# Projections from 128-row slices of x, transposed one piece at a time, and the leading maxima moved into the loop

## The chip, the core and the metric

The kernel runs on one core of a Trainium2 chip. Its engines each work through a queue of their own in order: TensorE (PE, with its weight loads shown as PEld), VectorE (DVE), ScalarE (ACT), GpSimd (POOL) and SyncE (SP), which here only issues transfers. The metric is the device time of one execution in microseconds; lower is better.

## The reference

Two independent halves, laid side by side in the output. The first is a state-space convolution: a long filter `K` is built from complex powers, and the input `u` is convolved with it by an FFT. The second is multi-head attention with 16 heads of 28 over 2048 positions.

```python
P = exp((A * dt[:, None])[:, :, None] * arange(2048))      # 448 x 256 x 2048, complex
K = 2 * einsum("dn,dnl->dl", C, P).real
a = irfft(rfft(u.T, 4096) * rfft(K, 4096))[:, :2048].T + u * D_skip

q, k, v = split_heads(x @ wqkv)       # x is 2048 x 448, wqkv is 448 x 1344
p = softmax(q @ k.T * 28 ** -0.5)
b = merge_heads(p @ v) @ wo
return concatenate([a, b], -1)
```

All numbers are float32.

## The kernel before

The kernel has a preamble and a loop.

The preamble makes q, k and v from x, and at the same time the seeds of the convolution's filter. x is cut in four quarters of 512 rows (`CQ`). For each quarter, `load_x` fetches two tiles `xn` (of three in all), `transposes` turns them on PE, and 12 jobs follow: eight `qk_proj` (four groups of heads, k and q each) and four `v_proj`. The width 448 is summed in four pieces of `CK` = 112 rows. PE multiplies in a fast float32 form, so each operand is split in a high and a low part. ACT copies the transposed piece from the PSUM tile `pt` (two buffers) into `xh`, rounded; DVE subtracts that from `pt` and writes the rest to `xl`. The weights are split in the same way (`w_g`, which lies in the memory that `khat` takes later, and `vh`, `vl`). A job adds up high times high, low weight times high x, and high weight times low x, for four pieces: twelve products into one PSUM bank `pm` (three banks in turn). After it ACT and DVE evacuate the bank into `hl` (or `vst`, or, for the last quarter's q, into the memory of `xn`), and SP stores it to DRAM. For k of the first two quarters there is a difference more, `kb` and `dhl`.

`seeds` makes the filter's seeds in eight rounds on ACT, DVE and POOL, with a few transposes (`pn`) on PE. The list `slots` sets how jobs and seed stages alternate as they are written down, 48 jobs in 37 slots (`PW`). In the preamble a planner then sets the order on each queue by its own costs (`KEPT["p"]` is empty); from the loop on every queue keeps the order as written (`KEPT["a"]`).

At the preamble's end, group 0's keys are loaded back as `khat` (and differences of keys as `kdif`), unit 0's queries as `qhat`, and the row maxima of unit 0 are taken. A unit is one group of four heads and one quarter of the queries; there are 16, and 16 steps of 128 keys each, so 256 steps. `max_put` sends the negated maxima `mh` into spare rows of `qhat`, so that the score products subtract them; ACT issues that transfer for unit 0.

Each step of the loop does, in the order of `ORDER`, four score products `pss` with their exponentials `p` on ACT, four products for the maxima of the next unit (`m0` to `m3`, `max_mm`), the product of p and v of the step before (`po`), and pieces of the convolution's work. A maximum's four products end in a ReLU `rl` on ACT for the first and a reduction on DVE for each of the other three. The loop runs `LEAD` = 3 steps ahead with its maxima; those three steps' twelve products stand between unit 0's maxima and the first step:

```python
for i in range(LEAD):
    for kc in range(4):
        max_mm(1, i, kc)
```

All instructions are recorded through one helper, so the profile puts them all on line 75; its rows are told apart by the tiles' names.

Of the kernel before, what the change touches and what calls it, by code (L numbers as in the profile page):

```python
# [18 lines left out]
D = 448  # L19

H = 16
DH = 28
# [2 lines left out]
CQ = 512  # L25
NQ = L // CQ
NK = L // 128
CK = 112
NCK = D // CK
SCALE = DH ** -0.5  # L30
NU = G * NQ
NS = NU * NK
# [6 lines left out]
SP, SH, PW, E3 = 4, 3, 37, 8  # L39
UG = (2, 2, 4)  # L40
PS = 1
SGB, XB, XL = 2, 5, 4
K0, KP, KD, UP = 0, 3.5, 4, 3
A0, A1 = 26, 31

# [45 lines left out]
def body(ctx, tc, a, out):  # L91
# [134 lines left out]
    with ExitStack() as st:  # L226
# [12 lines left out]
        def load_x(c):  # L239
            xs = x[c * CQ:(c + 1) * CQ, :].rearrange("(t p) d -> p t d", p=128)  # L240
            for h in range(2):
                xns[c, h] = y_p.tile([128, 2, CQ], F32, name="xn", bufs=3)[:, :, :D]
                nc.sync.dma_start(xns[c, h], xs[:, 2 * h:2 * h + 2, :])

        first = lambda o: (o // 4) * DF + (o % 4) * (JF // 4)
        nats = {}
# [47 lines left out]
                nc.vector.tensor_scalar(dt_all[:, i, :], dt_ps, f, None, op0=ALU.mult)  # L294

        load_x(0)
        w_g = k0_t[:CK].rearrange("p g (i s k h e) -> p i s k g h e", i=2, s=2, k=NCK, h=HG)
        vh = y_p.tile([CK, NCK, D], F32R, name="vh")
        vl = y_p.tile([CK, NCK, D], F32R, name="vl")
        nc.gpsimd.memset(k0_t[:CK].rearrange("p g (n e) -> p (g n) e", e=32)[:, :, DH:].bitcast(F32), 0.0)  # L300
# [4 lines left out]
        wns = []  # L305
        for i in range(2):
            wn = t_p.tile([128, 3, LV, BO * 16], F32, name="tri", bufs=2).rearrange("p t k h -> p (t k h)")
            wn = wn[:CK, :2 * 3 * D].rearrange("p (k s d) -> p k s d", k=2, s=3)
# [164 lines left out]

        def qk_proj(c, s, g):
            pp = w_tile()
            n = 0
            for k in range(NCK):
                for i, x_ in ((0, xh), (1, xh), (0, xl)):
                    nc.tensor.matmul(pp, w_g[:, i, s, k, g].rearrange("p h e -> p (h e)"), x_[k],
                                     start=n == 0, stop=n == 3 * NCK - 1)  # L480
                    n += 1

            def evac():
                if c == NQ - 1 and s == 0:
                    hl = y_p.tile([128, 2, CQ], F32, name="xn", bufs=3).bitcast(F32R)
                else:
                    hl = x_p.tile([128, 2, CQ], F32R, name="hl", bufs=3)
                th, tl = hl[:, 0], hl[:, 1]
                if s == 1:
                    nc.scalar.activation(th, pp, AF.Identity, bias=kones)  # L490
                    nc.vector.scalar_tensor_tensor(tl, pp, kones, th.bitcast(F32), op0=ALU.add, op1=ALU.subtract)
                else:
# [12 lines left out]
                nc.sync.dma_start((k_d[g][:, :, c * CQ:(c + 1) * CQ] if s == 1 else q_d[g][c]).rearrange("i p l -> p i l"),  # L505
                                  hl.bitcast(F32))
            return evac

        def v_proj(c, t):
            pp = w_tile()  # L510
            n = 0
            ts = slice(t * 128, (t + 1) * 128)
            for k in range(NCK):
                for w_, x_ in ((vh, xh), (vl, xh), (vh, xl)):
                    nc.tensor.matmul(pp[:, :D], x_[k][:, ts], w_[:, k, :], start=n == 0, stop=n == 3 * NCK - 1)
                    n += 1

            def evac():
                vs = vst[t % 2]
                nc.scalar.activation(vs[:, :, :DH], pp[:, :D].rearrange("p (h e) -> p h e", e=DH), AF.Copy)  # L520
                nc.sync.dma_start(v_d[c][:, :, t], vs.rearrange("p (g h) e -> p g (h e)", g=G))
            return evac

        work = []
        for c in range(NQ):
            jobs = [lambda c=c, s=s, g=g: qk_proj(c, s, g) for g in range(G) for s in (1, 0)]
            v_jobs = [lambda c=c, t=t: v_proj(c, t) for t in range(4)]
# [512 lines left out]
    def vec():  # L1040
        if powers["g"]:
            powers["g"].popleft()()

    prev = None
    for s in range(NS):
        u, kt = divmod(s, NK)
        sm = s + NK + LEAD
        if s == 12 * NK:
            k0_st.close()
            f_p["s", 0] = f_p["s", 1] = pool(f0_st, "f0_p", side="right")  # L1050
            f_ready["s", 0], f_ready["s", 1] = s, NS
# [20 lines left out]
        for op in ORDER:  # L1072
# [96 lines left out]
```

## Time and profile before

| | us |
|---|---|
| median of 3 runs (lowest to highest) | 1278.88 (1276.07 to 1279.31) |
| the profiled execution | 1278.37 |
| its span, first to last instruction | 1276.6 |
| PE busy in the span | 1223.9 (96%) |
| ACT, DVE, POOL busy | 967.5, 923.0, 846.2 |

Busy time counts an instruction from its start to its end. PE's products overlap one another, so a busy PE can still take more; how often products start tells more than how long one is. In the rows of the profile, `out<-in` are tiles, `[2.65 <-DVE xl L75]` means that the engine had stood idle for 2.65 us and what released it, and x4 means four instructions in a row. In the rows of waits stand the total in us, how often, and the longest.

### The profile page before, as it was taken

To read this page: it belongs to the slowest core of one execution; us is meant where nothing else is said; L and a number is where in the kernel's file an instruction comes from. 1 tells how busy PE (TensorE), PEld (TensorE's weight loads), DVE (VectorE), ACT (ScalarE), POOL (GpSimd) and SP (SyncE) were. 2 spreads that over 40 slices of the span, in tenths; PEclk is the share of its full clock that TensorE was granted. 3 is DMA by queue.
4 is the path that set the end of the run, shared out by engine and by line. 5 is a ranking of instruction groups with operands and counts; after the bars stand their busy time and mean duration, and the time that the engine had idled before them with its cause. 6 is when DMAs were issued, how large, how long until landed. Compare 5 with 4: busy or idle time off the path is not lost.

```text
span 1276.6 us, 33328 instructions
## 1 busy us (share of the span) xinstructions
PE 1223.9 (96%) x12641; PEld 699.3 (55%) x12641; DVE 923.0 (72%) x2106; ACT 967.5 (76%) x2162; POOL 846.2 (66%) x728
## 2 busy tenths in 40 slices
PE   7789887999999999999999999999999999999997
PEld 5667664555555555555555555555555545544433
DVE  6788866877777877877788888888897645645111
ACT  6878765788888888888878888888887666656452
POOL 2666750897788888878599999989995222324321
PEclk9889999899999999999999999999999999999999
DMA  7768699446564645375633133422324533657666
GB/s 216 244 223 288 233 304 346 113 93 186 160 149 113 168 119 168 113 235 167 176 94 104 49 88 97 154 81 71 88 54 156 179 131 135 204 170 228 198 170 167
DMA packets 200089, 205.36 MB, mean 161 GB/s; under 512 B 95992, under 2 KB 158520, under 8 KB 197880
## 3 DMA queue, kind: packets, MB, share of 16 engines
q1 hardware_dynamic: 199400, 202.63, 52.6%
q8 instruction: 100, 1.64, 0.5%
q10 hardware_dynamic: 528, 0.59, 0.2%
q14 instruction: 61, 0.50, 0.1%
HBM read 120.73 MB, written 82.18 MB: 159 GB/s over the span
## 4 chain that ended last, share of the span: by engine, by line
PE 75%; DVE 8%; POOL 6%; ACT 4%; issue 3%; DMA 3%; SPq 0%; ACTq 0%; POOLq 0%; DVEq 0%
PE pm L75 43%; PE pss L75 16%; PE po L75 16%; POOL e L75 2%; DVE tri L75 1%; ACT rl L75 1%; POOL qhat L75 1%; DVE mx L75 1%; DVE sg L75 1%; POOL eu L75 1%; ACT tri L75 1%; DVE px L75 1%; DVE qhat L75 1%; DVE hl L75 1%; DMA sd<-qhat 1%
## 5 line engine op out<-in xcount | busy, mean ns | idle before, releaser
L75 ACT ACTIVATE p<-pss 128x512 f32<-128x512 f32 x1024 | 561.0, 610 | 112.5 <-PE pss L75 107.2
L75 PE MATMUL pss<-qhat,khat 128*128 128x512 f32 x1024 | 403.2, 400 | 1.5 <-ACT p L75 1.4
L75 DVE TENSOR_REDUCE mx<-pm 128x1 f32<-128x512 f32 x480 | 308.6, 684 | 109.1 <-PE pm L75 107.2
L75 PE MATMUL pm<-khat,qhat 128*128 128x512 f32 x749 | 325.9, 438 | 6.4 <-ACT rl L75 4.2
L75 POOL TENSOR_TENSOR e<-e,sdb 128x256 f32<-128x256 f32 x168 | 201.8, 1201 | 110.6 <-ACT e L75 101.2
L75 PE MATMUL po<-p,v 128*32 128x512 f32 x2048 | 269.1, 594 | 0.0
L75 POOL TENSOR_TENSOR e<-e,eu 128x256 f32<-128x256 f32 x168 | 248.2, 1477 | 13.2
L75 PEld LDWEIGHTS pm<-khat,qhat 128*128 128x128 f32 x749 | 141.0, 189 | 201.9 <-ACT p L75 47.8
L75 DVE CUSTOM_DVE_ANT_0 rl<-pm,rl 128x512 f32<-128x512 f32 x259 | 178.3, 689 | 72.1 <-ACT rl L75 69.1
L75 PEld LDWEIGHTS pss<-qhat,khat 128*128 128x128 f32 x1024 | 190.6, 189 | 46.7 <-issue 10.8
L75 POOL TENSOR_TENSOR eu<-e,sdb 128x256 f32<-128x256 f32 x168 | 201.9, 1202 | 0.0
L75 POOL TENSOR_TENSOR p<-pr,pr 64x448 f32<-64x448 f32 x64 | 73.2, 1144 | 158.2 <-PE pm L75 132.8
L75 ACT ACTIVATE rl<-pm 128x512 f32<-128x512 f32 x259 | 156.6, 606 | 14.0 <-PE pm L75 8.4
L75 DVE TENSOR_TENSOR g<-g,zg 128x128 f32<-128x128 f32 x392 | 162.2, 414 | 3.4
L75 PE MATMUL pm<-kdif,qhat 128*128 128x512 f32 x249 | 100.5, 403 | 4.3 <-DVE xn L75 2.4
L75 PE MATMUL pm<-xh,khat 112*128 112x512 f32 x256 | 87.3, 425 | 4.9 <-DVE hl L75 1.8
L75 DVE TENSOR_TENSOR zg<-g,zg 128x128 f32<-128x128 f32 x224 | 88.0, 393 | 5.1
L75 PEld LDWEIGHTS pm<-e,g 128*32 128x32 f32 x3584 | 57.2, 109 | 43.4 <-issue 17.1
L75 DVE TENSOR_TENSOR pr<-pm,ub 128x448 f32<-128x448 f32 x64 | 37.0, 620 | 56.4 <-PE pm L75 42.0
L75 PE MATMUL pm<-e,g 128*32 128x64 f32 x3584 | 73.0, 222 | 1.8 <-POOL e L75 1.8
L75 ACT ACTIVATE y<-pm 128x448 f32<-128x448 f32 x48 | 26.5, 553 | 58.2 <-PE pm L75 36.2
L75 ACT ACTIVATE ub<-pm 128x224 f32<-128x224 f32 (+1 forms) x96 | 38.8, 449 | 39.7 <-PE pm L75 37.3
(134 smaller groups left out, 1461.8 us busy)
## 6 DMA issues: line engine op xcount, KB each, us to landing
sdb<-sd SPq DMA_DIRECT2D x55, 336.0 KB
qhat<-q SPq DMA_DIRECT2D x64, 256.0 KB
khat<-k SPq DMA_DIRECT2D x64, 256.0 KB
sd<-sg SPq DMA_DIRECT2D x8, 1456.0 KB
k<-hl SPq DMA_DIRECT2D x16, 512.0 KB
mw<-in_mw SPq DMA_DIRECT2D x16, 512.0 KB
sd<-qhat SPq DMA_DIRECT2D x8, 896.0 KB
yu_d<-ub SPq DMA_DIRECT2D x64, 112.0 KB
```

The costliest lines, as they stand in the source:

```text
L75: i = f(*args, **kw)
```

## The change

Three things are changed.

The width of 448 is now cut in three pieces of 128 rows and a rest of 64 (`TL`). The rest stands twice in a fourth piece of 128 rows: `load_x` fetches the last 64 columns of x a second time, behind the others, and the weights' last 64 rows are loaded twice. In the transposed fourth piece the lower half keeps the high part and the upper half is overwritten with the low part, so that one product with the high weights does high and low x together. A job then has 3 + 3 + 3 + 2 = 11 products.

The transposes of quarter c + 1 are written down piece by piece with jobs 7 to 10 of quarter c (`TJ`), not all ahead of the quarter's first job; only quarter 0 keeps them there. So x of two quarters is held at once: seven tiles a quarter, of which even quarters take five from the buffers of `v` (which the loop fills later), and the others come from `xt` (nine buffers, as many as `xh` and `xl` had together).

The leading maxima are no longer made ahead of the loop. `next_max` counts products, and a fifth one is made at the end of each step until the lead is reached, after step 11.

```diff
-CK = 112
-NCK = D // CK
+CK = 128
+NCK = 4
+TL = D - 3 * CK
-SGB, XB, XL = 2, 5, 4
+SGB, XT = 2, 9
+TJ = 7
...
             for h in range(2):
-                xns[c, h] = y_p.tile([128, 2, CQ], F32, name="xn", bufs=3)[:, :, :D]
-                nc.sync.dma_start(xns[c, h], xs[:, 2 * h:2 * h + 2, :])
+                xns[c, h] = y_p.tile([128, 2, CQ], F32, name="xn", bufs=3)
+                for d, n, at in ((0, D, 0), (D - TL, TL, D)):
+                    nc.sync.dma_start(xns[c, h][:, :, at:at + n], xs[:, 2 * h:2 * h + 2, d:d + n])
...
         for k in range(NCK):
-            nc.sync.dma_start(wns[k], wqkv[k * CK:(k + 1) * CK, :].rearrange("p (s d) -> p s d", s=3))
+            for p in range(1 if k < NCK - 1 else 2):
+                n = CK if k < NCK - 1 else TL
+                nc.sync.dma_start(wns[k][p * TL:p * TL + n], wqkv[k * CK:k * CK + n, :].rearrange("p (s d) -> p s d", s=3))
...
-        def transposes(c):
-            for k in range(NCK):
-                pt = ps_t.tile([128, CQ], F32, name="pt")[:CK]
+        def x_tile(c):
+            if c % 2:
+                return x_p.tile([128, CQ], F32R, name="xt", bufs=XT)
+            if n_x[0] < 5:
+                n_x[0] += 1
+                return v_p.tile([128, NK // NQ, HG, 32], F32, name="v", bufs=5).rearrange("p t h e -> p (t h e)").bitcast(F32R)
+            n_x[0] = (n_x[0] + 1) % 7
+            return x_p.tile([128, CQ], F32R, name="xt", bufs=XT)
+
+        def transposes(c, ks):
+            for k in ks:
+                pt = ps_t.tile([128, CQ], F32, name="pt")
                 for t in range(4):
                     nc.tensor.transpose(pt[:, t * 128:(t + 1) * 128], xns[c, t // 2][:, t % 2, k * CK:(k + 1) * CK], ident)
-                xh[k] = x_p.tile([CK, CQ], F32R, name="xh", bufs=XB)
-                xl[k] = x_p.tile([CK, CQ], F32R, name="xl", bufs=XL)
-                nc.scalar.activation(xh[k], pt, AF.Copy)
-                nc.vector.tensor_tensor(xl[k], pt, xh[k].bitcast(F32), ALU.subtract)
+                xh[c, k] = x_tile(c)
+                nc.scalar.activation(xh[c, k], pt, AF.Copy)
+                if k < NCK - 1:
+                    xl[c, k] = x_tile(c)
+                    nc.vector.tensor_tensor(xl[c, k], pt, xh[c, k].bitcast(F32), ALU.subtract)
+                else:
+                    nc.vector.tensor_tensor(xh[c, k][TL:], pt[TL:], xh[c, k][TL:].bitcast(F32), ALU.subtract)
...
-                for i, x_ in ((0, xh), (1, xh), (0, xl)):
-                    nc.tensor.matmul(pp, w_g[:, i, s, k, g].rearrange("p h e -> p (h e)"), x_[k],
+                for i, x_ in ((0, xh), (1, xh), (0, xl))[:3 if k < NCK - 1 else 2]:
+                    nc.tensor.matmul(pp, w_g[:, i, s, k, g].rearrange("p h e -> p (h e)"), x_[c, k],
...
-            jobs[0] = (lambda c, f: lambda: (transposes(c), f())[1])(c, jobs[0])
+            if c == 0:
+                jobs[0] = (lambda f: lambda: (transposes(0, range(NCK)), f())[1])(jobs[0])
             if c + 1 < NQ:
                 jobs[1] = (lambda c, f: lambda: (load_x(c + 1), f())[1])(c, jobs[1])
+                for k in range(NCK):
+                    jobs[TJ + k] = (lambda c, k, f: lambda: (transposes(c + 1, [k]), f())[1])(c, k, jobs[TJ + k])
...
-    for i in range(LEAD):
-        for kc in range(4):
-            max_mm(1, i, kc)
...
+    n_max = [4 * NK]
+
+    def next_max(end=None):
+        n = n_max[0]
+        if n < 4 * NS and (end is None or n < end):
+            n_max[0] += 1
+            max_mm(*divmod(n // 4, NK), n % 4)
...
+        lead = 4 * sm + 4 if s >= 4 * LEAD else 4 * (s + NK + 1) + s + 1
...
-            elif sm < NS:
-                max_mm(sm // NK, sm % NK, int(op[1]))
+            else:
+                next_max()
+        next_max(lead)
```

More of the change, by code (lines that the diff above doesn't have):

```diff
@@ L296, in body @@
         load_x(0)
-        w_g = k0_t[:CK].rearrange("p g (i s k h e) -> p i s k g h e", i=2, s=2, k=NCK, h=HG)
+        w_g = k0_t.rearrange("p g (i s k h e) -> p i s k g h e", i=2, s=2, k=NCK, h=HG)
         vh = y_p.tile([CK, NCK, D], F32R, name="vh")
         vl = y_p.tile([CK, NCK, D], F32R, name="vl")
-        nc.gpsimd.memset(k0_t[:CK].rearrange("p g (n e) -> p (g n) e", e=32)[:, :, DH:].bitcast(F32), 0.0)
+        nc.gpsimd.memset(k0_t.rearrange("p g (n e) -> p (g n) e", e=32)[:, :, DH:].bitcast(F32), 0.0)
         vst = [x_p.tile([128, H, 32], F32, name=f"vst{i}") for i in range(2)]
@@ L307, in body @@
             wn = t_p.tile([128, 3, LV, BO * 16], F32, name="tri", bufs=2).rearrange("p t k h -> p (t k h)")
-            wn = wn[:CK, :2 * 3 * D].rearrange("p (k s d) -> p k s d", k=2, s=3)
+            wn = wn[:, :2 * 3 * D].rearrange("p (k s d) -> p k s d", k=2, s=3)
             wns += [wn[:, 0], wn[:, 1]]
         for k in range(NCK):
-            nc.sync.dma_start(wns[k], wqkv[k * CK:(k + 1) * CK, :].rearrange("p (s d) -> p s d", s=3))
+            for p in range(1 if k < NCK - 1 else 2):
+                n = CK if k < NCK - 1 else TL
+                nc.sync.dma_start(wns[k][p * TL:p * TL + n], wqkv[k * CK:k * CK + n, :].rearrange("p (s d) -> p s d", s=3))
         pw2 = s_p.tile([128, LV], F32, name="pw2")
@@ L462, in body @@
         xh, xl = {}, {}
-        def transposes(c):
-            for k in range(NCK):
-                pt = ps_t.tile([128, CQ], F32, name="pt")[:CK]
+        def x_tile(c):
[6 more added lines that the diff above has]
+            return x_p.tile([128, CQ], F32R, name="xt", bufs=XT)
+        n_x = [0]
+        def transposes(c, ks):
+            for k in ks:
+                pt = ps_t.tile([128, CQ], F32, name="pt")
                 for t in range(4):
                     nc.tensor.transpose(pt[:, t * 128:(t + 1) * 128], xns[c, t // 2][:, t % 2, k * CK:(k + 1) * CK], ident)
-                xh[k] = x_p.tile([CK, CQ], F32R, name="xh", bufs=XB)
-                xl[k] = x_p.tile([CK, CQ], F32R, name="xl", bufs=XL)
-                nc.scalar.activation(xh[k], pt, AF.Copy)
-                nc.vector.tensor_tensor(xl[k], pt, xh[k].bitcast(F32), ALU.subtract)
+                xh[c, k] = x_tile(c)
[5 more added lines that the diff above has]
+                    nc.vector.tensor_tensor(xh[c, k][TL:], pt[TL:], xh[c, k][TL:].bitcast(F32), ALU.subtract)
         def qk_proj(c, s, g):
@@ L477, in qk_proj @@
             for k in range(NCK):
-                for i, x_ in ((0, xh), (1, xh), (0, xl)):
-                    nc.tensor.matmul(pp, w_g[:, i, s, k, g].rearrange("p h e -> p (h e)"), x_[k],
-                                     start=n == 0, stop=n == 3 * NCK - 1)
+                for i, x_ in ((0, xh), (1, xh), (0, xl))[:3 if k < NCK - 1 else 2]:
+                    nc.tensor.matmul(pp, w_g[:, i, s, k, g].rearrange("p h e -> p (h e)"), x_[c, k],
+                                     start=n == 0, stop=n == 3 * NCK - 2)
                     n += 1
@@ L513, in v_proj @@
             for k in range(NCK):
-                for w_, x_ in ((vh, xh), (vl, xh), (vh, xl)):
-                    nc.tensor.matmul(pp[:, :D], x_[k][:, ts], w_[:, k, :], start=n == 0, stop=n == 3 * NCK - 1)
+                for w_, x_ in ((vh, xh), (vl, xh), (vh, xl))[:3 if k < NCK - 1 else 2]:
+                    nc.tensor.matmul(pp[:, :D], x_[c, k][:, ts], w_[:, k, :], start=n == 0, stop=n == 3 * NCK - 2)
                     n += 1
```

## The prediction

> **What bounds the kernel now.** I read the granted clock over the span first, then the busy time by stage, then what TensorE waits for in the preamble, then the hand-over to the loop in order of time.
>
> ```profile
> PEclk9889999899999999999999999999999999999999
> ```
>
> Each digit is a slice of 32 us: the clock that PE was granted dips before the loop alone. The stages (columns: PE, PE's weight loads, DVE, ACT, POOL busy; PE clock; DMA share; GB/s):
>
> ```profile
> 11.00:56.00 45.00, 40.55 (x191) 32.38 (x192) 33.74 (x63) 38.48 (x92) 22.31 (x26) 1.00 0.71 218
> 56.00:101.00 45.00, 38.49 (x143) 30.16 (x142) 35.05 (x65) 34.23 (x88) 29.34 (x38) 0.77 0.70 243
> 101.00:168.00 67.00, 59.85 (x291) 47.21 (x289) 60.96 (x114) 57.32 (x146) 46.18 (x56) 1.00 0.81 272
> 168.00:187.00 19.00, 18.71 (x73) 14.77 (x73) 11.15 (x24) 9.32 (x20) 8.41 (x15) 0.91 0.84 271
> 187.00:219.00 32.00, 24.80 (x82) 14.37 (x81) 22.83 (x68) 21.23 (x39) 1.65 (x2) 0.95 0.96 347
> 219.00:229.00 10.00, 7.20 (x14) 3.83 (x15) 6.05 (x14) 2.41 (x6) 1.35 (x3) 0.55 0.88 283
> 229.00:277.00 48.00, 48.00 (x479) 25.84 (x478) 37.95 (x90) 39.85 (x90) 44.63 (x34) 0.99 0.38 94
> 281.00:1000.00 719.00, 713.88 (x8595) 399.20 (x8595) 588.25 (x1393) 599.13 (x1369) 604.49 (x474) 1.00 0.45 127
> ```
>
> The 48 projection jobs run from 11 to 187 us, unit 0's maxima to 219, the leading maxima to 229, then the loop. The loop is PE's (713.88 of 719), so whatever the loop gains at its start arrives at the end. In the preamble nothing is full: PE, DVE and ACT are busy 158, 141 and 139 of 176 us. But from 101 to 168 DVE has 60.96 of 67, 91%.
>
> **The change part by part.** *Products.* How often does PE start one?
>
> ```profile
> 27.32 0.40 PE L75 MATMUL pm<-xl,khat 112*128 112x512 f32 x1
> 27.56 0.62 PE L75 MATMUL pm<-xh,khat 112*128 112x512 f32 x2
> 28.02 0.40 PE L75 MATMUL pm<-xl,khat 112*128 112x512 f32 x1
> ...
> 41.33 0.36 PE L75 MATMUL pm<-vl,xh 112*128 112x448 f32 x1
> ...
> 41.73 0.36 PE L75 MATMUL pm<-vh,xh 112*128 112x448 f32 x1
> ```
>
> Three q/k products take 28.02 - 27.32 = 0.70 us, 0.233 each; two v products 0.40, 0.20 each (the 0.40 printed beside one is its length in a pipeline). Each of the 32 q/k jobs and 16 v jobs loses one of twelve: 32 x 0.233 + 16 x 0.20 = 10.7 us of PE at full clock. Their rows grow from 112 to 128; that costs nothing by these two rows (min/median/max ns):
>
> ```profile
> L75 PE MATMUL pm<-xh,khat x256: 388/394/775, 11.0 to 186.3; 112*128 112x512 f32 x128
> L75 PE MATMUL pt<-khat,qhat x19: 387/397/628, 190.1 to 215.6; 128*128 128x512 f32 x19
> ```
>
> *Transposes ahead.* Their number stays (64), as do 16 ACT copies and 16 DVE subtractions, four now on half the partitions. What goes is waiting, PE's in the preamble (total, times, longest):
>
> ```profile
> PE pt L75 <- DVE xl L75: 7.4, 5, 2.7
> PE pm L75 <- DVE hl L75: 6.8, 6, 2.6
> PE pn L75 <- ACT nat L75: 3.0, 2, 2.8
> PE pm L75 <- ACT xh L75: 0.7, 1, 0.7
> ```
>
> Two of the waits in the order of time:
>
> ```profile
> 9.27 1.10 PE L75 MATMUL pt<-ident,xn 128*112 128x128 f32 x4 [2.36 <-DVE xl L75]
> ...
> 60.83 1.10 PE L75 MATMUL pt<-ident,xn 128*112 128x128 f32 x4 [2.65 <-DVE xl L75]
> ```
>
> Of the 7.4 us, the first 2.36 belong to the first quarter, whose sixteen transposes still stand ahead of its products; 5.0 + 0.7 = 5.7 can go. The 6.8 us for `hl`, the evacuations on ACT and DVE, are late next.
>
> One wait costs more than itself:
>
> ```profile
> 56.00:66.00 10.00, 7.35 (x20) 5.36 (x19) 7.65 (x17) 5.90 (x19) 6.76 (x11) 0.51 0.95 306
> ```
>
> After 2.8 us for `nat`, and with the 2.65 us for `xl` in it, PE ran at half clock for 10 us. Without the second wait I let a third of that stretch go, 3.4 us, worth half, 1.7.
>
> *Weights and x.* The weights come as 512 rows, not 448, and each x half brings a second transfer of 64 columns:
>
> ```profile
> 10.00:18.00 8.00, 7.38 (x26) 5.37 (x25) 5.00 (x12) 5.72 (x12) 2.45 (x3) 1.00 1.00 205
> ...
> 16.36 1.05 ACT L75 ACTIVATE khat<-tri 112x448 fp32r<-112x448 f32 x2 [1.62 <-DMA tri<-in_B_wqkv]
> ...
> tri<-in_B_wqkv SPq DMA_DIRECT2D x4, 588.0 KB
> ```
>
> The DMA engines are full there, and ACT waits for weights at 16.36. 64 rows of 5376 bytes, 0.34 MB, and 0.07 MB of x at 205 GB/s make 2.0 us; ACT's other work in the queue hides a little, I take 1.8, bounds 0 and 3 (in the built program one more ACT copy of x, 0.6 us, stands ahead of the first weights' copy; it is in the upper bound). Of SP's nine new issues two stand ahead of the weights and one splits their last piece; the other six ride on a queue that waits for its producers anyway: 0. If it did not, an issue costs SP the 0.38 us of the `xn` row further down, 0.8 a quarter.
>
> *By stage.* 11 to 56 holds quarter 0: 8 x 0.233 + 4 x 0.20 = 2.7 off, 1.8 on: -0.9. 56 to 101 holds eight q/k products less (1.9), the wait of 2.65 and the 1.7 of clock, -6.2; DVE (78%) and ACT (76%) give part back, and x may be a little late (the rival on x below): -3.5 (bounds 0 and -10, where the whole cold stretch goes). From 101 to 168 twelve v and eight q/k jobs would save 4.3 and the other waits 3.0, but DVE's 60.96 us stand there; filled to 95% it takes 64.2: -2.8 (0 to -6). 168 to 187 is PE's own, DVE at 59%: 8 x 0.233 = -1.9. Sum -9.1.
>
> 187 to 219 keeps its work: 0. DMA is at 96% there, and four `khat` loads that don't come earlier cost up to +3.
>
> *Leading maxima.* Twelve products leave the gap between unit 0's maxima and the first score, and a fifth one stands at the end of steps 0 to 11.
>
> ```profile
> 219.38 2.01 ACTq L75 DMA_DIRECT2D qhat<-mh  x2
> 222.72 0.79 PE L75 MATMUL pm<-khat,qhat 128*128 128x512 f32 x1 [2.80 <-ACT rl L75]
> 224.40 0.81 SPq L75 DMA_DIRECT2D sdb<-sd  x2
> 227.08 0.41 ACT L75 ACTIVATE e<-sdb 128x256 f32<-128x256 f32 x1
> 227.39 0.31 ACT L75 ACTIVATE g<-sdb 128x128 f32<-128x128 f32 x1
> 228.65 0.63 PE L75 MATMUL pss<-qhat,khat 128*128 128x512 f32 x1
> 229.08 0.63 PE L75 MATMUL pm<-khat,qhat 128*128 128x512 f32 x1
> 229.38 0.59 ACT L75 ACTIVATE p<-pss 128x512 f32<-128x512 f32 x1
> 230.53 0.40 PE L75 MATMUL pm<-khat,qhat 128*128 128x512 f32 x1
> 230.76 0.40 PE L75 MATMUL pss<-qhat,khat 128*128 128x512 f32 x1
> ```
>
> The first score needs `mh` in `qhat`; behind that wait stands all of PE's queue. SP, which waited for that transfer, goes on at 224.40, so the score can start 4.25 us earlier. ACT has the `e` and `g` copies (0.72 us) and a `rl` queued ahead of the first exponential: I take 3.4 us as the shift. Twelve products in a PE-bound loop cost 12 x 0.233 = 2.8. DVE gets nine reductions more,
>
> ```profile
> L75 DVE TENSOR_REDUCE mx<-pm 128x1 f32<-128x512 f32 x480 | 308.6, 684 | 109.1 <-PE pm L75 107.2
> ```
>
> 6.2 us on its 37.95 of 48: 87% of 51, so 0, at worst +2. And the clock: at 228.65 products start 0.43 us apart, at 230.53 0.23. Now PE stands idle from about 219.4 to 224.4, with one maximum's product ahead of it, so step 0's nine products run at half speed instead of four: 5 x 0.2 = +1.0. In all -3.4 + 2.8 + 1.0 = +0.4, bounds -2 and +4.
>
> The Trainium skill ("TensorE: Matmul & The Clock Gate", section Part 1, on the HAM clock gate) says that the clock halves after an idle window of about 3.4 us and needs another 3.4 us of steady work to come back. By that rule alone the half clock would last to about 224.4 + 3.4 = 227.8, worth 1.7 us instead of the 0.8 it cost in the loop before: +0.9, and 1269.6 in the sum below. The trace agrees roughly (0.51 after waits of under 3 us, longer than one window), and the rule speaks against this part of the change and for the transposes.
>
> **Sum.** -9.1 + 0.4 = -8.7 on the profiled execution, whose own time is 1278.37 (span 1276.6; the median of the runs is 1278.88): 1269.7, say 1270.
>
> **Rivals.** *The wait moves to DVE and ACT.* If evacuations hold PE in every stage as they do from 101 to 168, only the product-bound last 1.9 us and a few waits remain: -3, 1275. For it: DVE at 91%, and `hl` as the second wait. Against: from 56 to 101 DVE has 10 us free.
>
> *All waits go.* Products 10.7, waits 5.7, and most of the preamble's half-clock time (0.23 of the 45 us from 56 to 101 is 10 lost, half of it recovered, 5), less 1.8 and 0.4: -19, 1259. For it: after each wait the clock fell. Against: DVE again.
>
> *x comes late (slower).* In the built program the third quarter's first transposes stand on PE after only three of the second quarter's jobs, earlier than job 7, with everything behind them in order, and its loads stand on SP behind the last v stores:
>
> ```profile
> 55.40 3.58 SPq L75 DMA_DIRECT2D v<-vst  x2
> 61.54 0.38 SPq L75 DMA_DIRECT2D xn<-in_B_x  x1
> ```
>
> Now the load starts at 61.54 and lands by about 64 (448 KB at 205 GB/s). The first quarter's last product starts at 49.92:
>
> ```profile
> 49.92 0.36 PE L75 MATMUL pm<-vh,xl 112*128 112x448 f32 x1
> ```
>
> Three jobs of eleven are 7.7 us, so PE can be there at 58 if banks are free, and waits 6, after which it runs cold for some two windows of 3.4 us, 3.4 lost. If the fourth quarter does the same, twice 9.4 are on: -8.7 + 18.8 = +10, 1288. Against: the banks come free with those same v evacuations, so PE is there later than 58 too. It decides from 6.3 us a quarter, a wait of 3 and the cold stretch behind it.
>
> *The planner undoes it*: transposes end up where they were, and the shorter jobs wait for the same evacuations: 1278.
>
> **Numbers.** Differences under 0.3% (3.8 us) can't be told from none here. Forecast 1270 (1265 to 1274) 0.45; wait moves 1275 (1273 to 1279) 0.22, a third of it under 1274.5; all waits go 1259 (1255 to 1263) 0.13; x late 1288 (1282 to 1292) 0.15; nothing 0.05. Faster 0.45 + 0.08 + 0.13 = 0.66, same 0.14 + 0.05 + 0.01 = 0.20, slower 0.14. 1260 to 1283 leaves out half of the outer two.
>
> **What would show it.** Products: 528 instead of 576, still 0.233 and 0.20 apart, the last job ending near 178 instead of 187. Transposes: PE's wait for `xt` under 2.5 us in all. Clock: 56 to 101 above 0.77. Loop: first score some 13 us earlier, step 0's products 0.43 apart, and 2.8 of it gone after step 11. It is wrong if DVE's idle time before `hl` grows by what PE loses, or if PE waits for `xn`.

## The result, and the profile after

The changed kernel takes 1283.12 us (median of 5 runs, 1283.03 to 1284.22) against 1278.99 for the kernel before (5 runs): a ratio of 1.0038, 95% interval 1.0027 to 1.0048. It is slower by 0.38%, where 1270 was forecast. The profiled span is 1282.2 us, 5.6 longer than the 1276.6 before.

The stages of the changed kernel, in the columns of the prediction's table (PE, PE's weight loads, DVE, ACT, POOL busy; PE clock; DMA share; GB/s):

```profile
11.00:56.00 45.00, 41.50 (x180) 32.58 (x179) 33.66 (x63) 37.15 (x89) 19.91 (x22) 0.92 0.64 200
56.00:101.00 45.00, 33.90 (x139) 27.04 (x138) 37.24 (x73) 37.98 (x97) 32.00 (x45) 0.85 0.78 267
101.00:168.00 67.00, 55.54 (x256) 45.29 (x255) 57.71 (x109) 55.33 (x142) 44.11 (x53) 0.92 0.78 262
168.00:187.00 19.00, 17.96 (x76) 13.81 (x74) 11.64 (x25) 9.09 (x19) 8.37 (x14) 1.00 0.87 278
```

PE is busy 4 us less from 101 to 168 (55.54 against 59.85) and as much less from 56 to 101, and yet the last projections are evacuated when they were before. First the kernel before, the last v and, behind the last octave's `sg` of the seeds, the last q:

```profile
170.16 0.55 ACT L75 ACTIVATE vst<-pm 128x448 f32<-128x448 f32 x1
...
187.76 0.57 ACT L75 ACTIVATE sg<-px 128x112 f32<-128x112 f32 x2 [2.03 <-DVE sg L75]
188.13 0.63 ACT L75 ACTIVATE xn<-pm 128x512 fp32r<-128x512 f32 x1
```

and the changed one:

```profile
171.71 0.52 ACT L77 ACTIVATE vst<-pm 128x448 f32<-128x448 f32 x1
...
187.67 0.57 ACT L77 ACTIVATE sg<-px 128x112 f32<-128x112 f32 x2 [1.51 <-DVE sg L77]
188.03 0.64 ACT L77 ACTIVATE xn<-pm 128x512 fp32r<-128x512 f32 x1
```

Between these marks the last stage is 17.97 - 16.32 = 1.65 us shorter, and all that lies ahead of it 1.55 longer: the preamble gained 0.1 us. These are single executions. Six kernels of the experiments (`maxima_only`, the two with the kinds kept, and the three in pieces) run the preamble in exactly the order of the kernel before, on every engine, and their last v is evacuated between 168.34 and 172.71 and their last q between 184.45 and 188.80; so what the parts give is read from the medians below, and not from a microsecond here. What PE waits for in the changed kernel's preamble (total, times, longest):

```profile
PE pm L77 <- DVE hl L77: 7.3, 6, 1.9
PE pt L77 <- DMA xn<-in_B_x: 6.7, 2, 5.5
PE pm L77 <- DVE kb L77: 5.5, 2, 3.5
PE pm L77 <- ACT vst L77: 4.8, 5, 2.4
PE pn L77 <- ACT nat L77: 4.2, 2, 3.9
PE pm L77 <- DVE xn L77: 3.0, 1, 3.0
...
PE pt L77 <- DVE xt L77: 1.4, 1, 1.4
...
PE pt L77 <- DVE v L77: 1.0, 1, 1.0
```

Rows of the kernel before that the prediction didn't show:

```profile
PE pt L75 <- DMA xn<-in_B_x: 4.7, 1, 4.7
...
PE pm L75 <- DVE xn L75: 2.4, 1, 2.4
PE pm L75 <- DVE kb L75: 1.4, 3, 0.9
PE pm L75 <- ACT vst L75: 1.1, 2, 1.0
```

The transposes' own waits fell from 8.1 us to 2.4 (`xt`, and 1.0 for the pieces held in v's tiles). Those for `kb`, `vst`, `nat` and both `xn` grew. (In the seven executions of the unchanged order `kb` stands at 1.4 to 1.5, `nat` at 3.0 and `vst` at 1.0 to 3.4.)

At the loop's start the first scores of steps 0, 1 and 13 show the rest. The changed kernel:

```profile
225.39 0.77 PE L77 MATMUL pss<-qhat,khat 128*128 128x512 f32 x1 [5.58 <-DMA qhat<-mh]
...
229.56 0.63 PE L77 MATMUL pss<-qhat,khat 128*128 128x512 f32 x1
...
283.86 0.39 PE L77 MATMUL pss<-qhat,khat 128*128 128x512 f32 x1
```

The kernel before, whose step 0 began at 228.65:

```profile
231.22 0.39 PE L75 MATMUL pss<-qhat,khat 128*128 128x512 f32 x1
...
277.24 0.40 PE L75 MATMUL pss<-qhat,khat 128*128 128x512 f32 x1
```

The first score is 3.26 us earlier. Step 0 then takes 4.17 instead of 2.57, and steps 1 to 12 together 54.30 instead of 46.02: 8.28 us more for eleven more products (steps 1 to 11), 0.75 each, three times the 0.233 of one product. By step 13 the lead of 3.26 has become a lag of 6.62, of which the span keeps 5.6.

### The profile page after: what moved, and what is told of

Its sections match the earlier page's. It is cut to its first block, busy times and chain, and to the rows that moved or that the text cites. A ratio compares the mean times of both kernels' runs of the same rounds, so it can differ in the third digit from the quotient of the medians.

```text
span 1282.2 us, 33252 instructions
## 1 busy us (share of the span) xinstructions
PE 1217.0 (95%) x12593; PEld 692.1 (54%) x12593; DVE 921.3 (72%) x2106; ACT 967.4 (75%) x2162; POOL 844.7 (66%) x728
## 4 chain that ended last, share of the span: by engine, by line
PE 76%; DVE 8%; POOL 4%; ACT 4%; issue 3%; DMA 3%; SPq 1%; ACTq 0%; POOLq 0%; DVEq 0%
PE pm L77 43%; PE pss L77 17%; PE po L77 16%; POOL e L77 1%; DVE mx L77 1%; DVE tri L77 1%; ACT rl L77 1%; SPq L77 1%; ACT tri L77 1%; DMA xn<-in_B_x 1%; PE pt L77 1%; POOL qhat L77 1%; DVE sg L77 1%; POOL p L77 1%; ACT p L77 1%
## 5 line engine op out<-in xcount | busy, mean ns | idle before, releaser
L77 PE MATMUL pm<-xt,khat 128*128 128x512 f32 x224 | 60.8, 419 | 9.1 <-ACT vst L77 2.8
```

What stands on the lines that cost most here:

```text
L77: i = f(*args, **kw)
```

## The experiments

Time is the median; "before" ran beside each group on the same chip (1278.1 to 1278.7). Where a step sum is given it is that from the first score of step 1 to that of step 13.

**Which part costs.** Four kernels take the change apart.

`maxima_only`: the kernel before, with

```diff
-    for i in range(LEAD):
-        for kc in range(4):
-            max_mm(1, i, kc)
...
-            elif sm < NS:
-                max_mm(sm // NK, sm % NK, int(op[1]))
+            else:
+                next_max()
+        next_max(lead)
```

> The kernel before with the third part alone: the leading maxima are made in the loop, one more product at the end of each of steps 0 to 11; x, the weights and the projections are as before. Theory 1 (crowding): the fifth product stands beside m2, m3 of its step and m0, m1 of the next; there the products come faster than DVE reduces (0.68 us each), PE waits for a bank, and each costs about 0.7 us: 12 x 0.7 = 8.5, less 3.3 for the earlier first score, +5: 1283 to 1285. Theory 2 (the loss comes with the other two parts, from what the preamble leaves behind on the queues): within 1.5 of 1279. The prediction's own sum for this part: +0.4, 1279.4.

Measured: 1284.96, ratio 1.0056 [1.0043, 1.0070]; steps 1 to 12 take 54.12. The third part is the whole loss, and theory 2 falls.

`slices_and_transposes_only`: the changed kernel with those lines undone.

> The changed kernel with the leading maxima back ahead of the loop, so parts one and two alone (128-row slices, eleven products, transposes piece by piece). Theory 1: the preamble isn't set by the number of products, its gain is nothing: 1277 to 1280. Theory 2: 1283. The prediction's own sum for these parts: -9, 1270.

Measured: 1278.01, ratio 1.0000 [0.9991, 1.0009]. The other two parts together are worth nothing.

`eleven_products_only`: the kernel before, with `CK = 128`, the four slices' loads and eleven products, and `transposes(c)` left in one block ahead of each quarter's first job:

```diff
-CK = 112
-NCK = D // CK
+CK = 128
+NCK = 4
+TL = D - 3 * CK
...
             jobs[0] = (lambda c, f: lambda: (transposes(c), f())[1])(c, jobs[0])
```

> The kernel before with the first part alone: slices of 128 rows and eleven products a job; the transposes stay in one block at each quarter's start, the leading maxima ahead of the loop. Theory 1 (the number of products doesn't set the preamble): 1277.5 to 1280.5. Theory 2 (it does, at least in the last stage, and the transposes moved ahead took the gain away): the last stage's 1.9 us and up to 9 of the 10.7 us that the products take, 1270 to 1277.

Measured: 1280.39, ratio 1.0022 [1.0012, 1.0033], at the upper end of theory 1 and rather a loss. So the transposes moved ahead come out about 2.4 us better on top (1280.39 to 1278.01), and the slices with their eleven products about as much worse (2.3), each in the order that the planner made for it.

`fifth_maximum_mid_step`: the changed kernel, with

```diff
                     if prev[1] == NK - 1:
                         fin(prev[0], s)
+                next_max(lead)
             else:
                 next_max()
-        next_max(lead)
```

(and `lead` lower by two, for m2 and m3 that now follow it).

> The changed kernel, but the additional product of steps 0 to 11 stands in the middle of the step, behind the product with v and ahead of the second slot of convolution work, away from the other four. Theory 1 (crowding): a bank is free there and DVE has time, each product costs PE 0.23 to 0.4 us instead of 0.7: 1283.1 - 4 to 5.5, 1277.5 to 1279.5. Theory 2 (a maximum more costs a DVE reduction wherever it stands, since DVE sets steps 0 to 11): 1282 to 1284.

Measured: 1284.03, ratio 1.0043 [1.0031, 1.0056], steps 1 to 12 in 53.64. My first theory, that the fifth product costs because it stands crowded beside the other four, fell.

**What a fifth product costs.** Two more places and orders, and then its cost in pieces. The first keeps m0 to m3 of each step as they were and takes the additional product from a list apart; the second does so in the step's middle:

```diff
+        if s < 4 * LEAD:
+            max_mm(1, s // 4, s % 4)
         for _ in range(FX if late[0] else 0):
```

> The kernel before with the leading maxima in the loop, but m0 to m3 of each step keep their own kinds and the additional product of steps 0 to 11 is taken from a list apart, at the step's end. Moving the fifth product to the step's middle cost as much as at its end, so crowding beside m0 to m3 isn't the cause by itself. Theory 3 (the kinds): in the kernel before, the product that ACT reads stands always in the same place, third of the four that lie together, and gives DVE 0.6 us; with the changed kernel's running list the kinds turn by one place a step, so that DVE reductions meet. With the kinds kept each product costs 0.25 to 0.4 us: 1285.0 - 4 to 5.5, 1279.5 to 1281. Theory 4 (a bank and a DVE reduction more in the ring of three banks, whatever their order): 1284 to 1286.

> As the run with the kinds kept, but the additional product in the middle of the step. Theory 3: like that run or a little better, 1278.5 to 1280.5. Theory 4: 1283 to 1286, as the running list in the middle of the step (1284.0).

Measured: 1284.57 (1.0051 [1.0038, 1.0065]; steps in 54.05) and 1283.84 (1.0050 [1.0037, 1.0063]; 52.67). Theory 3 falls. The order doesn't matter, and the place little: 0.60 us a product in the middle of the step against 0.73 at its end.

Then the pieces, without the twelve products ahead of the loop: a product that nobody reads, a reduction without a product, and a product issued again into the bank that m3 writes anyway:

```diff
+        if s < 4 * LEAD:
+            nc.tensor.matmul(w_tile(), q_u[1][:, 0, s // 4 * 128:s // 4 * 128 + 128], kt_g[0][0][:, s % 4 * CQ:(s % 4 + 1) * CQ], start=True, stop=True)
```

```diff
+        if s < 4 * LEAD:
+            nc.vector.tensor_reduce(m_u[1][:, 0, s // 4, 1:2], kt_g[0][0][:, s % 4 * CQ:(s % 4 + 1) * CQ].bitcast(F32), axis=AX.X, op=ALU.max)
```

```diff
-            nc.tensor.matmul(pm, q, kt[:, kc * CQ:(kc + 1) * CQ], start=True, stop=True)
+            for _ in range(2 if u == 1 and kc == 3 and i < 5 * LEAD else 1):
+                nc.tensor.matmul(pm, q, kt[:, kc * CQ:(kc + 1) * CQ], start=True, stop=True)
```

> The kernel before without the leading maxima, and in steps 0 to 11 a fifth product at the step's end whose bank nobody reads (the maxima of unit 1's first three row blocks are left out of the computation). It takes TensorE's time and a place in the ring of banks, but no DVE or ACT time. Without any cost of the loop the earlier first score would give 1278.1 - 3.3 = 1275. Theory 4 (what counts is that the reading engine gives the bank back late): 0.23 to 0.3 us each and about 1 us of half clock, 1278 to 1280. Theory 5 (TensorE alone: its 0.23 us and the pipeline's breaks between products cost 0.7 by themselves): 1284 to 1286.

> The kernel before without the leading maxima, and in steps 0 to 11 one more DVE reduction of 128x512 at the step's end, of an array in SBUF, with no product (the maxima of unit 1's first three row blocks are left out of the computation). Theory 4 in the form that DVE has free time (37.9 us busy of 48) and only the bank counts: 1275 to 1276. Theory 4 in the form that DVE's queue itself is the limit in these steps, each 0.68 us delaying all the reductions behind it, and with them the banks: 12 x 0.3 to 0.68, 1278.5 to 1283.

> The kernel before without the leading maxima (those of unit 1's first three row blocks are left out of the computation), and in steps 0 to 11 the product m3 is issued twice into the same bank, ahead of its one reduction: TensorE's work for a fifth product, but no place in the ring of three banks and no reader. The product without a reader, which had a place of its own, came to 1284.0, and m0 and m1 of the next step waited for the banks of m2 and m3, two places back instead of three. Theory 6 (the place in the ring costs more than half): 12 x 0.23 to 0.3 over the run with a reduction and no product (1277.4), 1280 to 1281.5. Theory 5 (TensorE's own time with its breaks is the whole cost): 1283 to 1285.

| additional in steps 0 to 11 | time, ratio | steps 1 to 12 | each of 11, over 46.02 |
|---|---|---|---|
| none (before) | 1278.1 to 1278.7 | 46.02 | |
| reduction alone | 1277.37, 0.9991 [0.9980, 1.0002] | 47.28 | 0.11 |
| product in m3's bank | 1278.84, 1.0003 [0.9994, 1.0011] | 48.59 | 0.23 |
| product with a bank, no reader | 1283.99, 1.0046 [1.0032, 1.0059] | 51.34 | 0.48 |
| product, bank and reader (`maxima_only`) | 1284.96, 1.0056 [1.0043, 1.0070] | 54.12 | 0.74 |

TensorE's time for the product is 0.23, as in the preamble. The place in the ring of three banks adds 0.25 although nobody reads it, and the reader 0.26 more, where a reduction by itself adds 0.11. The sizes are rough: in some of these traces step 1 begins at half clock (in `same_bank_twice` its first 1.3 us). From step 2 to step 12, at full clock in all of them, ten products cost 0.18, 0.46 and 0.74 us each and the reduction 0.13. Of the theories, the product without a reader (1283.99) came out at the edge of 5's range and not in 4's; `same_bank_twice` (1278.84) then ruled 5 out, and lies below theory 6's range as well; the reduction lies between its two. The product with a bank and the one without differ in their place in the step too (its end, and beside m3). A ring of four banks, the direct test, was not run. The place in the ring can be seen in the order of time, from m3 of one step to m1 of the next. `product_without_reader` (PE's rows; the additional product is the one at 255.32):

```profile
254.86 0.40 PE L75 MATMUL pm<-khat,qhat 128*128 128x512 f32 x1
255.10 0.39 PE L75 MATMUL pss<-qhat,khat 128*128 128x512 f32 x1
255.32 0.40 PE L75 MATMUL pm<-khat,qhat 128*128 128x512 f32 x1
255.58 0.50 PE L75 MATMUL pm<-kdif,qhat 128*128 128x512 f32 x1
255.91 0.40 PE L75 MATMUL pss<-qhat,khat 128*128 128x512 f32 x1
256.18 0.50 PE L75 MATMUL pm<-khat,qhat 128*128 128x512 f32 x1
256.51 0.40 PE L75 MATMUL pss<-qhat,khat 128*128 128x512 f32 x1
```

with, among its weight loads, those of m0 and m1, which stand behind a wait:

```profile
255.57 0.19 PEld L75 LDWEIGHTS pm<-kdif,qhat 128*128 128x128 f32 x1 [0.29 <-DVE mx L75]
...
256.18 0.19 PEld L75 LDWEIGHTS pm<-khat,qhat 128*128 128x128 f32 x1 [0.30 <-DVE mx L75]
```

`same_bank_twice`, where the additional product is the second of the two at 253.19:

```profile
253.19 0.63 PE L75 MATMUL pm<-khat,qhat 128*128 128x512 f32 x2
253.66 0.39 PE L75 MATMUL pss<-qhat,khat 128*128 128x512 f32 x1
253.88 0.40 PE L75 MATMUL pm<-kdif,qhat 128*128 128x512 f32 x1
254.12 0.39 PE L75 MATMUL pss<-qhat,khat 128*128 128x512 f32 x1
254.35 0.39 PE L75 MATMUL pm<-khat,qhat 128*128 128x512 f32 x1
```

With a place more between them, m0 needs the bank of m2 and m1 that of m3, whose reductions (0.68 each) have only just ended. m0 and m1 then start with their weights loaded late: the products behind them follow after 0.33 (255.58 to 255.91, 256.18 to 256.51) where 0.23 is usual. With the product in m3's own bank nothing waits, and all run 0.23 apart. The weight loads' waits for `mx` between 231 and 277 us, in the order before, changed, `product_without_reader`, `same_bank_twice`:

```profile
PEld pm L75 <- DVE mx L75: 3.3, 8, 0.8
```

```profile
PEld pm L77 <- DVE mx L77: 9.7, 23, 0.8
```

```profile
PEld pm L75 <- DVE mx L75: 6.0, 20, 0.4
```

```profile
PEld pm L75 <- DVE mx L75: 1.0, 3, 0.4
```

In the page of the changed kernel hardly any of this is idle time of PE (1.9 us for `mx` ahead of the products of `khat` and `qhat`, over the whole span), since a product's modelled length runs across the gap.

The run with a reduction alone also bounds what the third part could ever bring. With no additional product its first score is 3.65 us earlier (225.00 against 228.65) and that of step 13 1.20 (276.04 against 277.24); without the reductions' 1.26 it would be some 2.5. Twelve products at their bare 0.23 cost 2.8. This is one execution, and the first score of the kernels without the twelve products lies anywhere from 222.92 to 226.72.

**Why the preamble gave nothing.** All of the following stand on `slices_and_transposes_only` (1278.01). First TensorE's work, and the seeds':

```diff
-                for i, x_ in ((0, xh), (1, xh), (0, xl))[:3 if k < NCK - 1 else 2]:
+                for i, x_ in ((0, xh), (0, xl))[:2 if k < NCK - 1 else 1]:
...
-                for w_, x_ in ((vh, xh), (vl, xh), (vh, xl))[:3 if k < NCK - 1 else 2]:
+                for w_, x_ in ((vh, xh), (vh, xl))[:2 if k < NCK - 1 else 1]:
```

> Parts one and two (slices and transposes, leading maxima ahead of the loop; 1278.0), with seven products a job instead of eleven: those with the low half of the weights are left out of the computation, 128 x 0.233 + 64 x 0.20 = 42.6 us of TensorE's 176 in the preamble. Theory P (the number of products sets the preamble, and something else took the gain of the first step): 1236 to 1255. Theory S (the seeds' chain through ACT, DVE and POOL sets its pace, and TensorE only the last stage, from the last v product on): eight jobs of four products less there, 8 x 0.93 = 7.5, 1268 to 1276.

```diff
-            put_e = lambda: nc.sync.dma_start(sd_d[o][:, :, :F_G].rearrange("b p f -> p b f"), q["se"])
-            put_g = lambda: nc.sync.dma_start(sd_d[o][:, :, F_G:].rearrange("b p f -> p b f"), q["sg"])
+            if o % 2:
+                return [[] for _ in range(13)]
+            put_e = lambda: [nc.sync.dma_start(sd_d[i][:, :, :F_G].rearrange("b p f -> p b f"), q["se"]) for i in (o, o + 1)]
+            put_g = lambda: [nc.sync.dma_start(sd_d[i][:, :, F_G:].rearrange("b p f -> p b f"), q["sg"]) for i in (o, o + 1)]
```

> Parts one and two, but the seeds are worked out for the four even octaves alone, each stored twice (the odd octaves' seeds are left out of the computation); projections as they are. Theory S: TensorE finds its jobs' evacuations sooner and the preamble ends 10 to 40 us earlier, until TensorE's own 135 to 150 us of work set it: 1240 to 1268. Theory P: 1276 to 1279.

Measured: 1276.08 (0.9984 [0.9976, 0.9993]) and 1264.57 (0.9893 [0.9881, 0.9906]). 42.6 us of TensorE's work are worth 2, and half of the seeds 13.5. Theory P falls, and with it the prediction's first term; theory S holds for the seeds, but the whole gave 2 where S asked 7.5 of TensorE's own last stage alone. The preamble from 11 to 187 us, for `slices_and_transposes_only`, `seven_products` and `half_the_seeds` in turn:

```profile
11.00:187.00 176.00, 147.23 (x648) 117.38 (x646) 140.73 (x266) 139.74 (x346) 105.81 (x134) 0.93 0.76 252
```

```profile
11.00:187.00 176.00, 113.75 (x456) 85.90 (x455) 143.84 (x267) 142.27 (x351) 105.24 (x134) 0.83 0.77 255
```

```profile
11.00:187.00 176.00, 150.60 (x646) 119.46 (x645) 100.90 (x188) 102.39 (x233) 55.95 (x70) 0.92 0.82 276
```

With seven products PE is busy 114 of 176 us, and what it was relieved of it waits, or loses to the clock (0.83 against 0.93). From the waits of `seven_products`:

```profile
PE pn L77 <- ACT nat L77: 14.9, 6, 6.3
PE pm L77 <- DVE kb L77: 12.8, 4, 4.2
```

Its end shows one hand-over that eats a gain. PE's last q product ends at 177.35, in `slices_and_transposes_only` at 185.19. The evacuation of that job stands on ACT behind `sg` of the last octave, which waits for DVE, and comes only 3.0 us earlier (183.94 against 186.96):

```profile
181.48 0.57 ACT L77 ACTIVATE sg<-pn 128x112 f32<-128x112 f32 x2 [4.79 <-DVE px L77]
183.57 0.56 ACT L77 ACTIVATE sg<-px 128x112 f32<-128x112 f32 x2 [1.52 <-DVE sg L77]
183.94 0.63 ACT L77 ACTIVATE xn<-pm 128x512 fp32r<-128x512 f32 x1
```

The first score then comes 1.8 us earlier (226.77 against 228.60).

Next, one engine at a time relieved of a piece of the seeds:

```diff
-                act.activation(q["sn"], q["r"], AF.Sin, scale=TWO_PI)
-                act.activation(q["r"], q["r"], AF.Abs)
-                return act.activation(q["r"], q["r"], AF.Sin, scale=-TWO_PI, bias=half_pi)
+                return act.activation(q["r"][:, 0, :1], q["r"][:, 0, :1], AF.Copy)
```

> Parts one and two (1278.0), with ACT's sines left out of the seeds (three functions over 128x1232 an octave, 30.3 us in all, and most of the 17 table loads, 21.8 us): ACT loses some 50 of its 141 us in the preamble, each octave's chain about 5 us. Theory A (ACT's time holds the evacuations, and with them TensorE, back): 10 us off or more, 1255 to 1268. Theory D (DVE's time does): 1273 to 1279. Theory C (the length of each octave's chain through the engines does, whichever engine): in proportion to the chain, like the run without DVE's reduction but about twice as much, 1268 to 1275.

```diff
-            e5 = lambda: cmul(pol, e8(5, 8), e8(1, 4), 3, q["e8"][:, :, 0, :, 4], q["e8"][:, :, 1, :, 4], False)
+            e5 = lambda: [pol.memset(d, 0.0) for d in e8(5, 8)]
```

> Parts one and two, with POOL's products for three of the eight powers of e left out and zeros stored in their place (59.3 us of POOL's 106, at the chain's end, which nothing but the store to DRAM awaits). Theories A and D: 1276 to 1279. Theory C counts POOL only where another engine waits for it, and none waits for these: 1276 to 1279. If POOL or its stores set the pace: 1255 to 1270.

```diff
-                vec.tensor_scalar(q["sn"], q["r"], MAGIC, MAGIC, op0=ALU.add, op1=ALU.subtract)
-                vec.tensor_tensor(q["r"], q["sn"], q["r"], ALU.subtract)
+                vec.tensor_scalar(q["r"][:, 0, :1], q["r"][:, 0, :1], 0.0, None, op0=ALU.add)
...
-                act.activation(q["sn"], q["r"], AF.Sin, scale=TWO_PI)
+                act.activation(q["sn"], q["r"], AF.Sin, scale=1e-4)
                 act.activation(q["r"], q["r"], AF.Abs)
-                return act.activation(q["r"], q["r"], AF.Sin, scale=-TWO_PI, bias=half_pi)
+                return act.activation(q["r"], q["r"], AF.Sin, scale=1e-4)
```

> Parts one and two, with DVE's reduction of the phases left out (two operations over 128x1232 an octave, 19.9 us of DVE's 141 in the preamble, 2.5 us of each octave's chain). Theory D: 7 to 15 us off, 1263 to 1271. Theory A: 1275 to 1279. Theory C: 3 to 5 off, 1273 to 1275.

Measured: without ACT's sines 1280.90 (1.0021 [1.0012, 1.0030]), without POOL's powers 1272.98 (0.9959 [0.9946, 0.9972]), without DVE's reduction 1274.71 (0.9972 [0.9963, 0.9980]). Relieving ACT of some 47 us (it is busy 93.04 in the same stretch) made the kernel slower, which no theory had; theory A falls, and D got half of the least that it asked. POOL, which was to give nothing by all three, gave 5. C fits DVE's run (3.3, of 3 to 5), but not ACT's, which shortens the chain most. No single engine of these three sets the preamble's pace by its stock of work.

Last, the order. The jobs over 35 and over 38 stages, the third power on POOL (`E3 = 0`), and the transposes one job later (`TJ = 8`):

```diff
-SP, SH, PW, E3 = 4, 3, 37, 8
+SP, SH, PW, E3 = 4, 3, 35, 8
```

> Parts one and two, with the 48 jobs spread over 35 of the seeds' stages instead of 37, so that each is issued a little sooner. If shorter jobs can be used at all, then by letting them run ahead of the seeds. Theory S with seeds behind the last job that don't hold it up: 3 to 7 us off, 1271 to 1275. If the jobs wait for the same evacuations on ACT and DVE whatever their place in the order: 1277 to 1280.

> Parts one and two, with the 48 jobs spread over 38 of the seeds' stages instead of 37 (35 came to 1285.2, with the last octave's work, issued behind the last job, holding up SP's loads for unit 0's maxima). If that tail is what 37 still suffers from: 1274 to 1277. If 37 is where both end together: 1279 to 1284.

> Parts one and two (1278.0), with the third power of e worked out on POOL instead of DVE in all eight octaves: some 22 us of DVE's work in the preamble moved to POOL, which now waits 32 us for it, and two hand-overs an octave fewer. If the hand-overs and DVE's queue hold the octaves up: 1272 to 1276. If POOL's own time does (it gave 5 of 59 us when it was relieved): 1279 to 1290.

> Parts one and two, with the transposes of the next quarter spread over the last four jobs of a quarter, each a job later than in the changed kernel, so that they wait less for x (3.6 us of such waits behind the first, which belongs to the start). If these waits take the gain: 1274 to 1276.5. If the seeds' pace sets the time anyhow: 1277 to 1279.5.

Measured: 1285.20 (1.0060 [1.0048, 1.0072]), 1281.48 (1.0027 [1.0017, 1.0038]), 1280.36 (1.0012 [1.0003, 1.0021]) and 1283.60 (1.0038 [1.0024, 1.0052]). All are slower, both of the first two on either side of 37, and 35 and the transposes beyond what either theory allowed. Moving the transposes by one job costs some 5 us (1.0038 against 1.0000), where parts one and two together were forecast to bring 9.1. With 35 stages the loss lies behind the projections: the last q is evacuated at 187.84, 0.9 later than with 37, but PE then waits 8.9 us for the load of `qhat`, so this run doesn't tell whether shorter jobs can run ahead. The reading that fits the kernels of this group and the parts taken singly is that the order in which the planner puts five queues that wait for one another sets the preamble, and that each edit makes a new order; that is argued from them, not shown by one that changes the order alone.

What stays open: which hand-overs in that order carry the time, but for the one at the end shown above. A run whose order is frozen and whose work alone changes would be needed; it wasn't tried. No kernel here beats the kernel before with the whole computation in place.

## Why the prediction was wrong

**Products.** The step that failed is the one that let the saving count from 11 to 168. The prediction took PE's rate of 0.233 as the price of a product there; `seven_products` shows the price is near 2 / 192, 0.01 us. The last stage was not PE's own either. The 1.65 us by the marks above looks like the 1.9 forecast, but that is luck: in the profile of the kernel before PE had half clock from 168.8 to 172.2 (0.91 in the prediction's row), in the changed one it had not. The six kernels with the unchanged order, twelve products a job and no half clock there take 15.93 to 16.59 us between the same marks, no more than 16.32. PE itself did save what was forecast: from its last v product to its last q product it takes 21.9 us, against 23.9 in `maxima_only`. But the last evacuation, for which PE waits next (`xn`, 3.0), stands on ACT behind the seeds' `sg`, and came no earlier.

**Transposes ahead.** Right that their waits go: 5.7 of the 8.1 us went, and below the 2.5 that it named. Wrong that this time comes off. `kb`, `vst`, `nat` and `xn`'s load and evacuation took 4.1, 3.7, 1.2, 2.0 and 0.6 more, 11.6 together. The rival "the wait moves to DVE and ACT" had the mechanism, but its own price, 3 us off, still kept a gain.

**Clock.** From 56 to 101 it rose to 0.85, above the 0.77 named, but from 11 to 56 and from 101 to 168 it fell from 1.00 to 0.92. The sign that the prediction named tells nothing: with the preamble's order unchanged, `maxima_only` had 0.83 from 56 to 101 and 0.92 from 101 to 168, and `reduction_without_product` 0.90 and 0.97.

**Weights and x.** Priced at 1.8 with an upper bound of 3. The first q/k job is evacuated at 24.45 instead of 21.18, 3.3 later (the seven executions of the unchanged order lie between 20.25 and 22.19). The transfers are the smaller part: the last `khat` copies begin on ACT at 19.31 against 18.70. In the changed kernel the planner puts the first octave's phases on DVE ahead of the last weights' low halves, and PE waits:

```profile
21.89 1.44 DVE L77 TENSOR_TENSOR tri<-pn,pw 128x1232 f32<-128x1232 f32 x1
23.25 1.15 DVE L77 TENSOR_TENSOR khat<-tri,khat 128x448 fp32r<-128x448 f32 x2
...
23.91 1.04 PE L77 MATMUL pm<-xt,khat 128*128 128x512 f32 x3 [1.94 <-DVE khat L77]
...
24.45 0.69 ACT L77 ACTIVATE hl<-pm,kones 128x512 fp32r<-128x512 f32 x1
```

The prediction followed the DMA queue and ACT's work, and left DVE's order out. By the last v the changed kernel is 1.55 behind, which is within the spread of the unchanged order.

**By stage.** -0.9, -3.5 and -2.8 up to 168 came out as +1.55 together, -1.9 as -1.65 (not by the products, as said above); -9.1 became -0.1. The warning was in the prediction's own table: PE, DVE and ACT all stood between 79% and 90%, none full, in a stage whose order is planned. From 101 to 168 the 91% of DVE was read as room of 5% to fill; DVE now is at 57.71 of 67, 86%, and nothing was gained.

**x comes late, and the planner undoes it.** PE's two waits for `xn`, 5.5 and 1.2 us, both stand in the first 8 us of the kernel; the slower rival's 6 a quarter did not come. The time on which "nothing" was put, 1278, is what parts one and two gave, but the transposes did stay ahead.

**Leading maxima.** The first score was to come 4.25 us earlier and the first exponential 3.4. They came 3.26 and 1.91 earlier:

```profile
227.47 1.07 ACT L77 ACTIVATE p<-pss 128x512 f32<-128x512 f32 x2
```

against 229.38 before. The wait for `mh` and the half clock in step 0 (its first products 0.43 apart) were right; step 0 grew by 1.6 where 1.0 + 0.23 was forecast. The step that failed is "twelve products in a PE-bound loop cost 12 x 0.233 = 2.8", with DVE "0, at worst +2": eleven cost 8.28. DVE's busy share, 87%, was the wrong number to look at. What a product more takes in this loop is a bank of three, for as long as a reader behind other work on an in-order engine needs, and the next two maxima wait for it. The three prices were 0.23 (TensorE), 0.25 (the place) and 0.26 (the reader).

**The clock gate.** PE starts again at 225.39, and this stretch shows half clock from there on:

```profile
225.40:230.50 5.10, 5.10 (x12) 3.44 (x12) 2.83 (x8) 4.03 (x10) 3.38 (x5) 0.50 0.76 220
230.60:231.00 0.40, 0.40 (x6) 0.16 (x8) 0.40 (x3) 0.30 (x2) 0.40 (x1) 1.00 0.56 139
```

That is at least 5.1 us, not the 3.4 that the prediction added to the restart. The Trainium skill ("TensorE: Matmul & The Clock Gate", Part 1) says that the activity window is free-running and doesn't start with the work; a restart in the middle of a window then pays the rest of it and a whole one, by an estimate from the page's 3.4 us anything from 3.4 to 6.8. The changed kernel's trace agrees with that reading (5.1), and the prediction had used the page's other sentence alone. The kernel before doesn't fit it: PE started again at 222.72 and had half clock until 230.2, 7.5 us, with products about 0.6 us apart that waited for their banks. Why is open.

## What to carry to other kernels

Price an additional product by what it takes besides TensorE's time: a place in the ring of banks brings each later tenant one release nearer, and the reader holds it; a full in-order loop charged 0.74 us for a product of 0.23. Where several engines stand near 80% and a planner sets the order, a saving on one of them isn't worth its length: leave out several times as much first, and see whether the end moves (here 43 us of TensorE moved it by 2). And weigh both ends of a move: ahead of the loop the twelve products cost 3.3 us, 0.27 each, so that in the loop even their bare 0.23 could hardly have earned anything.

## What the runs showed that was not expected

A weight load that has to wait, even 0.3 us, costs the product it belongs to: 0.33 us to the next instead of 0.23, though the profile counts PE as busy throughout. A tile that is written and never read cost the loop as much again as its product (0.48 against 0.23). Leaving out some 47 us of ACT's work in the preamble made the kernel 0.2% slower. And seven executions of one and the same order of instructions ended the projections anywhere from 184.45 to 188.80, with the stretches of half clock in different places, so that a change of a few microseconds can't be read from one profile of this stage.
